# Routing made for nine tiles of two batches at once, and tail results in other PSUM banks, in a fused retention and mixture-of-experts kernel

## The chip, the cores and the metric

The kernel runs on one core of one Trainium2 chip. The metric is the device time of one execution in microseconds (us): 628.96, the median of three runs (627.0 to 629.3).

## The reference, cut to what matters

Decayed attention without a softmax over 8 batches of 8 heads (576 positions, width 64), then a layer in which every one of the 4608 tokens goes to one expert of eight:

```python
scores = scale * np.matmul(q, k.transpose(0, 1, 3, 2))
Dmat = np.where(rel >= 0, gamma[:, None, None] ** rel[None, :, :], 0.0)
attn = np.matmul(scores * Dmat[None], v)
x = attn.transpose(0, 2, 1, 3).reshape(4608, 512)
logits = (x / norm(x)) @ (emb / norm(emb)).T / tau
expert_idx = np.argmax(logits, axis=1)        # and a gate weight by softmax
h = np.maximum(x[mask] @ w1[e], 0.0)
out[mask] = gate_w[mask, None] * (h @ w2[e])  # for each expert e
```

## The kernel before

The first 170 us compute the attention, batch by batch, and route the tokens on the side; the rest are the experts, one after the other. Python loops are unrolled, and a scheduler lays out one fixed instruction order for each engine. An engine works its queue in order, so an instruction that waits holds all that stand behind it.

**A round** is here one pass `b` of the batch loop; it has four steps `p`, one for each pair of heads. The text counts a round from the end of the last tail (`emit_Ot`) to the end of the next. In each round TensorE (PE) does:

- `emit_A(b, p)`: scores of a pair, into two PSUM banks of the pool `psa` (three banks, tile `a`). VectorE (DVE) multiplies them by the causal mask and writes them to SBUF (L599, tile `raw`).
- `emit_QT` and `emit_O`: the carried state and the scores times the values, both into a bank of `pso` (two banks, tile `o`, called `PO[p]`). DVE evicts it in `emit_X` (L681, L683, L684).
- At the end of a round (`p` = 3): the next batch's first scores, `emit_At` (scores of the 64 tail positions, evicted by DVE into `pt`, L695), `emit_U` (the next batch's states, two banks, evicted by DVE into `Tst`, L627 and L629), the last `emit_O`, and `emit_Ot` (the tail's output, two half banks for even and odd pairs, evicted by L722). In the version before, `emit_At`, `emit_U` and both halves of `emit_Ot` take banks of `psm` (three banks, tile `m`).

**Routing.** 576 tokens of a batch are 4.5 tiles of 128, so an even batch has 4 tiles and an odd one 5. For each batch `route_logits`, `route_tile` (transposes, ScalarE (ACT) evicts, the rows go to DRAM) and `route_turn` run in the slots after steps 0 and 2 of the round behind it. `route_head` (six small DVE instructions: maximum, one-hot of the expert), `route_rank` (matmuls with triangle and ones, then DVE), `route_onehot` (three wide DVE instructions `ra`, `bt`, `rp`) and `route_table` (one matmul for each tile) turn logits into a table of which token lies in which slot of which expert. In the version before each of these runs once for each batch: head of batch `b` in round `b`+1, its rank, one-hots and table in round `b`+2. In round 7 a list of tasks does what is left of batches 5 and 6, and `slots_to_tokens` and three `gather`s of tokens for the first expert.

**Beside it.** GpSimd (POOL) scales the next batch's values (L567, L571) once they have landed. In rounds 2 to 5 one quarter of the first expert's weights is loaded (`wsplit_tasks`), cast by ACT (L168) and its rest formed by DVE (L169). Loads wait for free buffers; all go through the queue of SyncE.

Of the kernel before, what the change touches and what calls it, by code (L numbers as in the profile page):

```python
# [18 lines left out]
P = 128  # L19
# [6 lines left out]
NE = 8  # L26
# [60 lines left out]
def retention_moe(ctx: ExitStack, tc: tile.TileContext, qk, kv, embT, tau, w1, w2, cst, out):  # L87
# [89 lines left out]

    def group_tiles(b):
        t0 = (b // 2) * 9 + (0 if b % 2 == 0 else 4)
        return t0, (4 if b % 2 == 0 else 5)  # L180

    def route_head(b):

        t0, G = group_tiles(b)
        L = L_all[:, t0 : t0 + G, :]

        def bc(x):
            return x.unsqueeze(2).broadcast_to([P, G, NE])

        def bce(x):  # L190
            return x.unsqueeze(1).broadcast_to([P, G, NE])

        mx = sm.tile([P, 5], F32, name="mx")[:, :G]
        nc.vector.tensor_reduce(out=mx, in_=L, axis=AX.X, op=ALU.max)
        nc.vector.tensor_tensor(out=L, in0=L, in1=bc(mx), op=ALU.subtract)
        w = sm.tile([P, 5, NE], F32, name="w")[:, :G]
        nc.vector.scalar_tensor_tensor(out=w, in0=L, scalar=0.0, in1=bce(wme), op0=ALU.is_ge, op1=ALU.mult)
        wm = sm.tile([P, 5], F32, name="wm")[:, :G]
        nc.vector.tensor_reduce(out=wm, in_=w, axis=AX.X, op=ALU.max)
        oh = sm.tile([P, 5, NE], BF16, name="oh")[:, :G]  # L200
# [42 lines left out]
    def route_rank(b):  # L243
# [9 lines left out]
        mm(r, stri, oh, start=True, stop=False)  # L253
        if b > 0:
            mm(r, ones, bce(run), start=False, stop=False)
# [4 lines left out]
        nc.vector.tensor_reduce(out=s1, in_=oh.rearrange("p g e -> p e g"), axis=AX.X, op=ALU.add)  # L260
        if b == 0:
# [4 lines left out]
        t1 = sm.tile([P, 5, NE], F32, name="t1")[:, :G]  # L266
        nc.vector.tensor_tensor(out=t1, in0=r, in1=oh, op=ALU.mult)
# [5 lines left out]

        si = sm.tile([P, 5], I32, name="si")[:, :G]
# [3 lines left out]
        ai = sm.tile([P, 2, 5], I32, name="ai")[:, :, :G]  # L278
        nc.vector.tensor_scalar(out=ai[:, 0], in0=si, scalar1=7, scalar2=None, op0=ALU.logical_shift_right)
# [3 lines left out]
    def route_onehot(b):  # L283

        t0, G = group_tiles(b)
        ai = grp[b][0]
        bt = sm.tile([P, 5, P], BF16, name="bt", bufs=1)[:, :G]
        nc.vector.tensor_tensor(
# [4 lines left out]
        )  # L293
        ra = sm.tile([P, 5, NE, CT], F32, name="ra", bufs=1)[:, :G]
        held = cc("iota")[:, : NE * (CT + 1)].rearrange("p (e i) -> p e i", e=NE)[:, :, :CT]
# [5 lines left out]
        )  # L301
        rp = sm.tile([P, 5, 2, NA], BF16, name="rp", bufs=1)[:, :G]
        nc.vector.tensor_tensor(
# [7 lines left out]
    def route_table(b):  # L311
# [11 lines left out]
        u = ps[:, : 2 * NA].rearrange("p (k a) -> p k a", k=2)  # L323
        if b == 0:
# [122 lines left out]
    with ExitStack() as att:  # L447
# [238 lines left out]
        def emit_At(b):  # L686
            ps = psm.tile([P, 512], F32, name="m")
            u = ps[:, : NP * TL].rearrange("p (r n) -> p r n", r=NP)
# [44 lines left out]
        def route_tile(b, g):  # L733

            t0, G = group_tiles(b)
            src = tile_src(b, g)
# [29 lines left out]
        def route_turn(b):  # L766
            t0, G = group_tiles(b)
            lt = ltb.pop(b)
# [399 lines left out]
```

## Time and profile before

| | |
|---|---|
| median of three runs | 628.96 us (627.0 to 629.3) |
| the profiled execution, own time | 627.92 us |
| its span, first to last instruction | 626.1 us |
| PE busy | 609.4 us (97%) |
| DVE busy | 339.3 us (54%) |
| ACT, POOL busy | 216.7 us, 180.3 us |
| rounds 1 to 7 (29.16 to 166.64 us) | 137.48 us, PE busy 129.36 |
| granted TensorE clock, whole span | 0.995 of full |

Times below are us from the start of the span. A line of a timeline or of a table of waits says in brackets how long the engine sat idle in front of the instruction, and what released it. Matmul ends are modelled, so a busy PE need not be at its peak rate.

### The profile page before, as it was taken

The numbers are of one execution on the slowest core, as the hardware profiler recorded it, in microseconds if no ns is written. First come the engines' busy times: TensorE is split into PE (matmuls) and PEld (weight loads), VectorE is DVE, ScalarE is ACT, GpSimd is POOL, SyncE is SP. The second block draws the span as 40 slices with busy tenths as digits, with TensorE's granted clock in tenths as the row PEclk, the third lists the DMA queues.
The fourth block names the chain that finished last, engine by engine and source line by source line (L and its number), as shares of the span: only waits on it lengthen the run. The fifth ranks groups of instructions, "written<-read, shape, count | busy, mean of one in ns | idle before, by whom it ended". The sixth has DMA issues, their size and how long they took to land. (4 is left out here: it accounts for less than half of the span.)

```text
span 626.1 us, 12659 instructions
## 1 busy us (share of the span) xinstructions
PE 609.4 (97%) x5273; PEld 541.6 (87%) x5273; DVE 339.3 (54%) x687; ACT 216.7 (35%) x397; POOL 180.3 (29%) x165
## 2 busy tenths in 40 slices
PE   9999999989899999999999999999999999999995
PEld 8877778867698989889988998998899899889985
DVE  5676877768767776723670673368057426802200
ACT  1033333423444554423351433335143333512211
POOL 2522022220156636032313504241341324020011
PEclk9999999989999999999999999999999999999999
DMA  8899887972367895661483258147324824510001
GB/s 308 311 329 367 300 317 275 344 262 103 106 208 218 206 307 153 149 235 46 118 274 103 81 115 268 65 118 238 130 69 114 273 71 117 149 51 9 2 35 44
DMA packets 73275, 109.41 MB, mean 175 GB/s; under 512 B 44634, under 2 KB 45054, under 8 KB 71424
## 3 DMA queue, kind: packets, MB, share of 16 engines
q1 hardware_dynamic: 65536, 88.63, 44.1%
q0 software_dynamic: 7680, 19.95, 9.6%
q8 instruction: 42, 0.69, 0.4%
q14 instruction: 17, 0.14, 0.1%
HBM read 79.96 MB, written 19.94 MB: 160 GB/s over the span
## 5 line engine op out<-in xcount | busy, mean ns | idle before, releaser
L109 PE MATMUL a<-xs,wslot 128*128 128x384 f32 (+1 forms) x1536 | 227.8, 309 | 0.0
L109 PEld LDWEIGHTS a<-xs,wslot 128*128 128x128 f32 x1536 | 225.8, 189 | 0.7
L913 PE MATMUL o<-wslot,hs 128*128 128x512 f32 (+1 forms) x984 | 222.0, 386 | 0.0
L913 PEld LDWEIGHTS o<-wslot,hs 128*128 128x128 f32 x984 | 181.1, 188 | 38.3
L887 DVE SCALAR_TENSOR_TENSOR hs<-a,hs 128x384 fp32r<-128x384 f32 (+1 forms) x128 | 62.8, 490 | 170.6 <-ACT hs L886 167.8
L921 POOL DMA_INDIRECT out<-y,sid x40 | 43.4, 1086 | 225.1 <-ACT y L920 192.8
L886 ACT ACTIVATE hs<-a 128x384 fp32r<-128x384 f32 (+1 forms) x128 | 56.1, 439 | 127.3 <-PE a L109 117.3
L169 DVE TENSOR_TENSOR wslot<-raw,wslot 128x1024 fp32r<-128x1024 f32 x64 | 78.3, 1223 | 26.5 <-ACT wslot L168 25.4
L168 ACT CAST wslot<-raw 128x1024 fp32r<-128x1024 f32 x64 | 66.8, 1044 | 39.2 <-DMA raw<-w 39.2
L355 POOL DMA_INDIRECT raw<-xd,gid x40 | 41.6, 1041 | 88.8 <-DVE wslot L169 45.6
L920 ACT ACTIVATE y<-o,gt 128x512 f32<-128x512 f32 (+1 forms) x41 | 27.7, 677 | 110.5 <-PE o L913 94.7
L567 POOL TENSOR_TENSOR vt<-vt,cs 128x512 f32<-128x512 f32 x28 | 28.3, 1045 | 90.4 <-DMA vt<-kv 74.4
L366 POOL DMA_INDIRECT gt<-gd,gid x40 | 50.0, 1251 | 12.2 <-issue 12.2
L109 PE MATMUL a<-qkt 64*128 64x128 f32 x512 | 43.0, 291 | 2.5 <-DVE raw L599 2.5
L599 DVE TENSOR_TENSOR raw<-a,tri 128x512 f32<-128x512 f32 x64 | 41.4, 684 | 6.1 <-PE a L109 6.0
L109 PEld LDWEIGHTS a<-qkt 64*128 64x128 f32 x512 | 34.9, 189 | 7.5 <-DVE raw L599 3.9
L109 PE MATMUL o<-raw,vt 128*64 128x128 f32 x512 | 36.1, 280 | 0.0
L109 PEld LDWEIGHTS o<-raw,vt 128*64 128x64 f32 x512 | 28.2, 138 | 4.3 <-issue 3.2
L400 DVE COPY raw<-raw 128x1024 uint16<-128x1024 uint16 x37 | 28.2, 785 | 4.0 <-DMA raw<-raw 4.0
L744 ACT COPY y<-m 128x512 f32<-128x512 f32 x34 | 18.8, 586 | 32.5 <-PE m L113 32.4
L393 DVE COPY raw<-raw 128x1024 uint16<-128x1024 uint16 x37 | 26.0, 717 | 0.9 <-DMA raw<-xd,gid 0.9
L763 ACT COPY lt<-m 128x512 f32<-128x512 f32 (+1 forms) x12 | 5.4, 482 | 59.8 <-PE m L109 59.8
(127 smaller groups left out, 386.6 us busy)
## 6 DMA issues: line engine op xcount, KB each, us to landing
raw<-w SPq DMA_DIRECT2D x64, 512.0 KB, 4.8
qkt<-qk SPq DMA_DIRECT2D x32, 576.0 KB, 6.4
xd<-y SPq DMA_DIRECT2D x36, 256.0 KB, 3.5
vt<-kv SPq DMA_DIRECT2D x7, 1152.0 KB, 10.3
kt<-kv SPq DMA_DIRECT2D x7, 1024.0 KB, 5.0
vt<-kv SPq DMA_DIRECT2D x4, 256.0 KB
raw<-xd,gid POOLq DMA_INDIRECT x40
gt<-gd,gid POOLq DMA_INDIRECT x40
```

Of the source, the lines that this page charges most:

```text
L109: pe[:] = [nc.tensor.matmul(*args, **kw)]
L168: nc.scalar.copy(hi, raw)
L169: nc.vector.tensor_tensor(out=sl[:, 1, c * 1024 : (c + 1) * 1024], in0=raw, in1=hi.bitcast(F32), op=ALU.subtract)
L355: return nc.gpsimd.indirect_dma_start(out=t[:, :DM], out_offset=None, in_=xd[:rows, :], in_offset=bass.IndirectOffsetOnAxis(ap=gid[:, a : ...
L366: nc.gpsimd.indirect_dma_start(out=g[:, i : i + 1], out_offset=None, in_=gd[:, :], in_offset=bass.IndirectOffsetOnAxis(ap=gid[:, a : a + 1 ...
L400: nc.vector.tensor_copy(far.bitcast(U16).rearrange("p (n h) -> p h n", h=2), near.rearrange("p (h n) -> p h n", h=2))
L567: eng.tensor_tensor(out=v[:, c], in0=v[:, c], in1=g[:, c].unsqueeze(2).broadcast_to([P, H, D]), op=ALU.mult)
L599: nc.vector.tensor_tensor(out=pm[:, h], in0=ps[h].rearrange("p (c n) -> p c n", c=NCH), in1=tri.unsqueeze(1).broadcast_to([P, NCH, P]), op ...
L886: a = nc.scalar.activation(hi, ps[:, :n], AF.Relu)
L887: v = nc.vector.scalar_tensor_tensor(out=hs[:, 1, f, o : o + n], in0=ps[:, :n], scalar=0.0, in1=hi.bitcast(F32), op0=ALU.max, op1=ALU.subt ...
L913: nc.tensor.matmul(ps[:, :step], hs[:, hsp, f, i * P : (i + 1) * P], w[:, ws, f, n : n + step], start=(f == 0 and k == 0), stop=(f == NF - ...
L921: nc.gpsimd.indirect_dma_start(out=out[:, :], out_offset=bass.IndirectOffsetOnAxis(ap=sid[:, a : a + 1], axis=0), in_=y, in_offset=None, b ...
```

## The change

Batches are routed in pairs. `group_tiles` now gives the nine tiles of two batches to head, rank, one-hots and table, for batches 0 to 5; batches 6 and 7 stay single. The work that a batch does for itself (`route_tile`, `route_turn`) asks `batch_tiles`. So head runs in rounds 2, 4 and 6 for nine tiles, and rank, one-hots and table in rounds 3, 5 and 7 for nine tiles; rounds 1, 3 and 5 have no head, and rounds 2, 4 and 6 no rank, one-hots or table. The tail scores of `emit_At` take a bank of `psa`, and the odd half of `emit_Ot` one of `pso`.

```diff
+    def batch_tiles(b):
         t0 = (b // 2) * 9 + (0 if b % 2 == 0 else 4)
         return t0, (4 if b % 2 == 0 else 5)
+    def group_tiles(b):
+        return batch_tiles(b) if b >= B - 2 else ((b // 2) * 9, 9)
...
-        mx = sm.tile([P, 5], F32, name="mx")[:, :G]
+        mx = sm.tile([P, 9], F32, name="mx")[:, :G]
...
-        if b > 0:
+        if b > 1:
             mm(r, ones, bce(run), start=False, stop=False)
...
         def emit_At(b):
-            ps = psm.tile([P, 512], F32, name="m")
+            ps = psa.tile([P, 512], F32, name="a")
...
             for odd in range(2):
-                ps = psm.tile([P, 512], F32, name="m")
+                ps = pso.tile([P, 512], F32, name="o") if odd else psm.tile([P, 512], F32, name="m")
...
-            own = [lambda: route_logits(b)] + tiles[:2], tiles[2:] + [lambda: route_turn(b), head]
+            own = [lambda: route_logits(b)] + tiles[:2], tiles[2:] + [lambda: route_turn(b)] + [head] * (b % 2)
             first, second = owed or ([], [])
-            owed[:] = [rank], [table]
+            owed[:] = ([rank], [table]) if b % 2 else ()
```

The order of instructions at three places follows. On DVE, at the end of round 1, before: the head of batch 0 (`mx` to `tok_all`, and the sums `s` and `run`) stands between the logits and the first scores of batch 2 (`raw`).

```order
L776 TENSOR_REDUCE L_all<-m 128x32
L194 TENSOR_REDUCE mx<-L_all 128x4
L195 TENSOR_TENSOR L_all<-L_all,mx 128x32
L197 SCALAR_TENSOR_TENSOR w<-L_all,wme 128x32
L199 TENSOR_REDUCE wm<-w 128x4
L201 TENSOR_TENSOR oh<-wm,wme 128x32
L202 TENSOR_SCALAR tok_all<-wm 128x4
L260 TENSOR_REDUCE s_874<-oh 128x8
L262 CAST run<-s_874 128x8
L599 TENSOR_TENSOR raw<-a,tri 128x512 x2
L695 TENSOR_TENSOR pt<-m,trit 128x256
```

Scores and `pt` stand behind the whole head. The same place in the change (line numbers are four higher):

```order
L780 TENSOR_REDUCE L_all<-m 128x32
L603 TENSOR_TENSOR raw<-a,tri 128x512 x2
L699 TENSOR_TENSOR pt<-a,trit 128x256
L631 COPY Tst_196<-m 128x256
L633 TENSOR_TENSOR Tst_196<-m,Tst_196 128x256 x3
```

The eight instructions of head and sums are gone from here; scores and `pt` follow the logits at once.

On DVE at the end of round 3, in the change (before, the head of batch 2 stood between the table's eviction and L169):

```order
L780 TENSOR_REDUCE L_all<-m 128x32
L329 COPY tab<-m 128x80
L169 TENSOR_TENSOR wslot_81<-raw,wslot_81 128x1024
L603 TENSOR_TENSOR raw<-a,tri 128x512 x2
L699 TENSOR_TENSOR pt<-a,trit 128x256
L631 COPY Tst_196<-m 128x256
L633 TENSOR_TENSOR Tst_196<-m,Tst_196 128x256 x3
L687 TENSOR_TENSOR xC<-o,gsb 128x64
L688 TENSOR_TENSOR xT<-o,gsb 128x448
L726 TENSOR_TENSOR xT<-m,gsb 128x2x64
L726 TENSOR_TENSOR xT<-o,gsb 128x2x64
```

The head has left; L169 (the rest of the weights) still stands in front of the scores, `pt`, the states, the last `emit_X` and the two tail evictions, of which the second now reads a bank of `pso`.

On PE, from the end of round 4 on, before (`m_1651` are the tail scores, `m_1662` the first bank of the states, `m_1709` and `m_1710` the two halves of the tail):

```order
L109 MATMUL m_1651<-qkt_1105 64x64 [waits DVE_49]
...
L109 MATMUL m_1662<-vt_1412,kt_1414 64x64 [waits DMAHW7_49,Activation_49,Pool_49]
...
L109 MATMUL o_1559<-raw_1555,vt_1107 64x128 x8
L109 MATMUL m_1709<-qkt_1105,Tst0_196 64x64 [waits DVE_49]
L109 MATMUL m_1709<-qkt_1105,Tst0_196 64x64
L109 MATMUL m_1710<-qkt_1205,Tst0_196 64x64 [waits DVE_49,PE_49]
```

The states wait for a load, ACT and POOL, and both halves of the tail for DVE. The same place in the change (`a_1581` are the tail scores, `m_1592` the states, `m_1639` and `o_1640` the halves of the tail, `pt_1590` the masked tail scores):

```order
L109 MATMUL a_1581<-qkt_1067 64x64 [waits DVE_49]
...
L109 MATMUL m_1592<-vt_1371,kt_1373 64x64 [waits DMAHW7_49,DVE_49,Pool_49]
...
L109 MATMUL o_1495<-raw_1491,vt_1069 64x128 x8
L109 MATMUL m_1639<-qkt_1067,Tst0_196 64x64 [waits Activation_49]
L109 MATMUL m_1639<-qkt_1067,Tst0_196 64x64
L109 MATMUL o_1640<-qkt_1170,Tst0_196 64x64 x2
L109 MATMUL m_1639<-pt_1590,vt_1069 64x64 [waits DVE_49]
```

The states no longer wait for ACT, the odd half of the tail waits for no bank, and the wait for DVE has moved to the first matmul that reads `pt`.

On PE at the start of round 2, the first `emit_QT`, before (`o_811` and `o_812` are its two banks):

```order
L109 MATMUL o_812<-qkt_593,Tst0_196 64x128 [waits DVE_49,PE_49]
L109 MATMUL o_812<-qkt_593,Tst0_196 64x128
L109 MATMUL o_811<-qkt_517,Tst0_196 64x128 x2
L109 MATMUL o_812<-qkt_593,Tst0_196 64x128 x2
L109 MATMUL o_811<-raw_705,vt_519 64x128 x8
```

The only bank to be waited for was the one that is written first. The same place in the change (`o_801` and `o_802` are the two banks):

```order
L109 MATMUL o_801<-qkt_517,Tst0_196 64x128 [waits DVE_49,PE_49]
L109 MATMUL o_801<-qkt_517,Tst0_196 64x128
L109 MATMUL o_802<-qkt_593,Tst0_196 64x128 [waits DVE_49]
L109 MATMUL o_802<-qkt_593,Tst0_196 64x128
L109 MATMUL o_801<-qkt_517,Tst0_196 64x128 x2
L109 MATMUL o_802<-qkt_593,Tst0_196 64x128 x2
```

Now both banks are waited for: `o_802` is the one that the odd half of the tail has just used, and DVE must have evicted it (L726, the second). The same stands at the start of rounds 3 to 6.

## Rows read from the trace of the kernel before

**Rows 1.** The windows of the seven rounds, PE alone: window, its length, PE busy (instructions), granted TensorE clock as a share of full speed, DMA share, GB/s; the last row is the sum.

```profile
29.16:47.96 18.80, 17.35 (x321) 1.00 0.91 332
47.96:67.66 19.70, 19.10 (x340) 1.00 0.83 301
67.66:87.69 20.03, 18.33 (x330) 1.00 0.88 331
87.69:107.72 20.03, 19.11 (x341) 1.00 0.82 303
107.72:127.96 20.24, 18.33 (x330) 1.00 0.79 302
127.96:148.64 20.68, 20.32 (x341) 0.92 0.66 235
148.64:166.64 18.00, 16.82 (x263) 1.00 0.37 123
sum 137.48, PE 129.36; mean PE 18.48
```

**Rows 2.** A window in the experts' part, all engines: length, then busy time (instructions) of PE, PE's weight loads, DVE, ACT and POOL, granted clock, DMA share, GB/s.

```profile
300.00:400.00 100.00, 100.00 (x553) 90.56 (x552) 47.91 (x69) 35.52 (x59) 28.96 (x26) 1.00 0.54 155
```

**Rows 3.** What PE waited for in the seven rounds (29 to 166.7 us): the tile of the waiting matmul and its line, what released it; then us in total, times, the longest.

```profile
PE m L109 <- DVE pt L695: 2.6, 3, 1.0
PE a L109 <- DVE raw L599: 1.9, 5, 0.4
PE m L109 <- issue: 1.7, 4, 0.6
PE m L109 <- DVE Tst L629: 1.7, 3, 0.6
```

**Rows 4.** PE's timeline at the ends of rounds 1, 3 and 5, the first matmuls of `emit_Ot`: start, length, instruction, idle time in front and its releaser.

```profile
46.47 0.33 PE L109 MATMUL m<-qkt,Tst 64*64 64x64 f32 x4 [0.88 <-DVE pt L695]
...
86.20 0.33 PE L109 MATMUL m<-qkt,Tst 64*64 64x64 f32 x4 [0.75 <-DVE pt L695]
...
126.47 0.33 PE L109 MATMUL m<-qkt,Tst 64*64 64x64 f32 x4 [0.96 <-DVE pt L695]
```

**Rows 5.** DVE's instructions by shape, 30 to 150 us, one of the head: line, operation, tiles, out<-in, count | busy us, mean ns of one | idle us in front. 128x32 is a head of 4 tiles, 128x40 one of 5.

```profile
L197 DVE SCALAR_TENSOR_TENSOR w<-L_all,wme 128x32 f32<-128x32 f32 x3 | 2.5, 824 | 0.1
...
L197 DVE SCALAR_TENSOR_TENSOR w<-L_all,wme 128x40 f32<-128x40 f32 x3 | 0.6, 191 | 0.0
```

**Rows 6.** POOL's timeline in round 1, the scaling of the next batch's values.

```profile
39.92 4.05 POOL L567 TENSOR_TENSOR vt<-vt,cs 128x512 f32<-128x512 f32 x4 [15.96 <-DMA xd<-y]
```

**Rows 7.** Timelines of ACT and DVE at the end of round 3: the cast of the weights, their rest, `pt`, the evictions of the tail; and the cast in round 4.

```profile
82.31 1.05 ACT L168 CAST wslot<-raw 128x1024 fp32r<-128x1024 f32 x1 [0.77 <-DMA raw<-w]
83.39 1.23 DVE L169 TENSOR_TENSOR wslot<-raw,wslot 128x1024 fp32r<-128x1024 f32 x1
85.73 0.41 DVE L695 TENSOR_TENSOR pt<-m,trit 128x256 f32<-128x256 f32 x1
88.37 0.48 DVE L722 TENSOR_TENSOR xT<-m,gsb 128x128 f32<-128x128 f32 x2
101.69 1.05 ACT L168 CAST wslot<-raw 128x1024 fp32r<-128x1024 f32 x1 [0.85 <-DMA raw<-w]
```

**Rows 8.** PE's timeline, the first `emit_QT` of round 4.

```profile
88.78 0.34 PE L109 MATMUL o<-qkt,Tst 64*64 64x128 f32 x4
```

**Rows 9.** The timeline of SyncE's queue at the ends of rounds 2 and 3: the loads of the next queries and keys, which wait for the buffers that `emit_Ot` reads. Then two windows of PE, columns as in rows 1.

```profile
67.13 0.81 SPq L457 DMA_DIRECT2D qkt<-qk  x2
86.57 1.20 SPq L457 DMA_DIRECT2D qkt<-qk  x2
69.00:82.00 13.00, 12.60 (x187) 1.00 1.02 405
104.00:107.00 3.00, 3.00 (x84) 1.00 0.23 88
```

**Rows 10.** PE's timeline, the states (`emit_U`) at the end of round 4.

```profile
103.93 2.09 PE L109 MATMUL m<-vt,kt 128*64 128x64 f32 x64 [0.56 <-issue]
```

**Rows 11.** PE's timeline, a wait of the scores (`emit_A`) in round 6.

```profile
137.87 1.16 PE L109 MATMUL a<-qkt 64*128 64x128 f32 x14 [0.36 <-DVE raw L599]
```

**Rows 12.** PE's timeline in round 3: the rank's matmuls with `ones`, and the table's, for 5 tiles.

```profile
72.57 0.24 PE L109 MATMUL m<-oh,ones 128*128 128x32 bf16 x4
80.51 0.34 PE L109 MATMUL m<-rp,bt 128*128 128x80 bf16 x5
```

**Rows 13.** DVE's timeline in round 3, the one-hots of 5 tiles.

```profile
73.73 0.37 DVE L296 TENSOR_TENSOR ra<-ai,cs 128x200 f32<-128x200 int32 x1
74.01 0.82 DVE L288 TENSOR_TENSOR bt<-ai,cs 128x640 bf16<-128x640 int32 x1
74.75 0.57 DVE L303 TENSOR_TENSOR rp<-ra,entry 128x400 bf16<-128x400 f32 x1
```

**Rows 14.** A window in round 6, all engines, columns as in rows 2.

```profile
130.00:131.00 1.00, 1.00 (x24) 0.72 (x16) 0.95 (x2) 0.00 (x0) 0.00 (x0) 0.50 0.92 336
```

**Rows 15.** Round 7, timelines of DVE, POOL and PE: the list of slots turned into token numbers, the gather's three issues, the first transposes of gathered tokens.

```profile
160.95 0.17 DVE L340 CAST gid<-t 128x3 int32<-128x3 f32 x1
162.01 1.19 POOL L355 DMA_INDIRECT raw<-xd,gid  x1 [20.09 <-DVE raw L599]
166.64 1.39 PE L113 MATMUL m<-ident,raw 128*128 128x128 f32 x8
```

More of the change, by code (lines that the diff above doesn't have):

```diff
@@ L176, in retention_moe @@
     grp = {}
-    def group_tiles(b):
+    def batch_tiles(b):
         t0 = (b // 2) * 9 + (0 if b % 2 == 0 else 4)
         return t0, (4 if b % 2 == 0 else 5)
+    def group_tiles(b):
+        return batch_tiles(b) if b >= B - 2 else ((b // 2) * 9, 9)
     def route_head(b):
@@ L191, in bce @@
             return x.unsqueeze(1).broadcast_to([P, G, NE])
-        mx = sm.tile([P, 5], F32, name="mx")[:, :G]
+        mx = sm.tile([P, 9], F32, name="mx")[:, :G]
         nc.vector.tensor_reduce(out=mx, in_=L, axis=AX.X, op=ALU.max)
         nc.vector.tensor_tensor(out=L, in0=L, in1=bc(mx), op=ALU.subtract)
-        w = sm.tile([P, 5, NE], F32, name="w")[:, :G]
+        w = sm.tile([P, 9, NE], F32, name="w")[:, :G]
         nc.vector.scalar_tensor_tensor(out=w, in0=L, scalar=0.0, in1=bce(wme), op0=ALU.is_ge, op1=ALU.mult)
-        wm = sm.tile([P, 5], F32, name="wm")[:, :G]
+        wm = sm.tile([P, 9], F32, name="wm")[:, :G]
         nc.vector.tensor_reduce(out=wm, in_=w, axis=AX.X, op=ALU.max)
-        oh = sm.tile([P, 5, NE], BF16, name="oh")[:, :G]
+        oh = sm.tile([P, 9, NE], BF16, name="oh")[:, :G]
         nc.vector.tensor_tensor(out=oh, in0=bc(wm), in1=bce(wme), op=ALU.is_equal)
@@ L260, in route_rank @@
         nc.vector.tensor_reduce(out=s1, in_=oh.rearrange("p g e -> p e g"), axis=AX.X, op=ALU.add)
-        if b == 0:
+        if b == 1:
             nc.vector.tensor_copy(run, s1)
@@ L265, in route_rank @@
         rk = rank_all[:, t0 : t0 + G]
-        t1 = sm.tile([P, 5, NE], F32, name="t1")[:, :G]
+        t1 = sm.tile([P, 9, NE], F32, name="t1")[:, :G]
         nc.vector.tensor_tensor(out=t1, in0=r, in1=oh, op=ALU.mult)
@@ L272, in route_rank @@
         nc.vector.tensor_reduce(out=rk, in_=t1, axis=AX.X, op=ALU.add)
-        si = sm.tile([P, 5], I32, name="si")[:, :G]
+        si = sm.tile([P, 9], I32, name="si")[:, :G]
         nc.vector.scalar_tensor_tensor(
@@ L277, in route_rank @@
         )
-        ai = sm.tile([P, 2, 5], I32, name="ai")[:, :, :G]
+        ai = sm.tile([P, 2, 9], I32, name="ai")[:, :, :G]
         nc.vector.tensor_scalar(out=ai[:, 0], in0=si, scalar1=7, scalar2=None, op0=ALU.logical_shift_right)
@@ L286, in route_onehot @@
         ai = grp[b][0]
-        bt = sm.tile([P, 5, P], BF16, name="bt", bufs=1)[:, :G]
+        bt = sm.tile([P, 9, P], BF16, name="bt", bufs=1)[:, :G]
         nc.vector.tensor_tensor(
@@ L293, in route_onehot @@
         )
-        ra = sm.tile([P, 5, NE, CT], F32, name="ra", bufs=1)[:, :G]
+        ra = sm.tile([P, 9, NE, CT], F32, name="ra", bufs=1)[:, :G]
         held = cc("iota")[:, : NE * (CT + 1)].rearrange("p (e i) -> p e i", e=NE)[:, :, :CT]
@@ L301, in route_onehot @@
         )
-        rp = sm.tile([P, 5, 2, NA], BF16, name="rp", bufs=1)[:, :G]
+        rp = sm.tile([P, 9, 2, NA], BF16, name="rp", bufs=1)[:, :G]
         nc.vector.tensor_tensor(
@@ L323, in route_table @@
         u = ps[:, : 2 * NA].rearrange("p (k a) -> p k a", k=2)
-        if b == 0:
+        if b == 1:
             nc.vector.tensor_copy(tab, u)
@@ L733, in route_tile @@
         def route_tile(b, g):
-            t0, G = group_tiles(b)
+            t0, G = batch_tiles(b)
             src = tile_src(b, g)
@@ L766, in route_turn @@
         def route_turn(b):
-            t0, G = group_tiles(b)
+            t0, G = batch_tiles(b)
             lt = ltb.pop(b)
@@ L786, in route_tasks @@
         def route_tasks(b):
-            G = group_tiles(b)[1]
+            G = batch_tiles(b)[1]
             tiles = [lambda g=g: route_tile(b, g) for g in range(G)]
@@ L797, in route_tasks @@
                 t += tiles[2:] + [table, lambda: slots_to_tokens(0, 3)]
-                t += [lambda i=i: gather(0, i, group_tiles(B - 1)[0] * P) for i in range(3)]
+                t += [lambda i=i: gather(0, i, batch_tiles(B - 1)[0] * P) for i in range(3)]
                 return t + [route_bump]
```

## The prediction, blind

> **What bounds the kernel now.** I read the windows first. In the experts' part PE has no gap (100.00 busy of 100.00, clock 1.00 [rows 2]), so whatever the rounds lose or gain is carried to the end. The rounds last 137.48 us, with PE busy 129.36 of it [rows 1]; the 8.1 us between are what the change can reach, with the part of round 6 that ran at a lower clock. Next, the table of waits: four lines make nearly all of the 8.1, the tail waiting for `pt` (2.6), the tail's odd half (1.7), the states (1.7, shown as "issue") and the scores waiting for `raw` (1.9) [rows 3]. Last, the timelines of these places, to see what made the releaser late. At the ends of rounds 1, 3 and 5 PE idles 0.88, 0.75 and 0.96 us in front of `emit_Ot` [rows 4].
>
> Rounds 2 to 5 have a second limit beside PE. DMA is full for most of a round (1.02 at 405 GB/s from 69 to 82 us) and nearly idle at its end (0.23) [rows 9], because the next loads of queries and keys wait for buffers that `emit_Ot` reads. These loads are issued at 67.13 and 86.57, and the cast of the weights, which waits for its own load behind them, starts at 82.31 and 101.69 [rows 7, 9]: 15.18 and 15.12 us later, twice the same. From the cast (82.31) a solid chain of DVE runs through L169 (83.39), scores, `pt` (85.73), states and `emit_X` to the tail's eviction, which ends at 88.85, 6.54 us behind the cast [rows 7]; at 88.78 the next `emit_QT` starts [rows 8]. So a round of this kind is held by three things: PE's program, "the next `emit_QT` not before cast + 6.5", and "the cast 15.1 behind the last `emit_Ot`'s first loads".
>
> **The change part by part.** All terms are against the profiled execution, 627.92 us, which lies 1.04 below the median of 628.96.
>
> *End of round 1.* The head of 4 tiles goes from in front of `pt`. It ran beside POOL's scaling (39.92, 4.05 us in four pieces [rows 6]), and one of its operations took 824 ns, where that of 5 tiles takes 191 [rows 5]. Without it `pt` is ready before PE comes: −0.88 [rows 4]. The odd half gets a bank of its own: its wait (1.7 for three times [rows 3], 0.57 each) goes as well. There is no weight cast in this round. PE comes to the next `emit_QT` earlier by all of it: −1.45. Cover: the new wait of `emit_QT` for the odd half's eviction is hidden by the first scores of the next batch, about as long as PE ran there between tail and `emit_QT` (1.1 us, 87.69 to 88.78 [rows 1, 8]).
>
> The Trainium skill (SBUF — State Buffer, Who interferes with whom) says that a VectorE operation with two SBUF inputs and a GpSimd operation that reads SBUF take the shared port pair as an exclusive lock for a whole instruction; 824 against 191 ns agrees. By that rule a nine-tile head that met the scaling in round 6 would be held by some 0.63 us in each of its three such operations, 1.9 in all, and the sum would be −1.8 instead of −3.7; the five-tile heads of rounds 2, 4 and 6, in whose place it stands, did not meet it.
>
> *Rounds 2 to 5, PE's side.* It offers the waits for `pt` of rounds 3 and 5 (0.75, 0.96 [rows 4]) and twice 0.57 of the odd half; the states no longer wait for ACT's copy, of which 0.56 shows at the end of round 4 [rows 10]; and with no one-hots in rounds 2 and 4 the scores there don't wait for `raw` (up to 0.4 each [rows 3]). Work moves from rounds 2 and 4 to 3 and 5: rank and table of 4 tiles on PE, 0.2 + 0.25 us by the rows of 5 [rows 12], no net cost. The one-hots of 5 tiles take 0.37 + 0.82 + 0.57 = 1.76 us [rows 13]; of nine at most 9/5 of that, so DVE's block grows by up to 1.4 in rounds 3 and 5. PE has an `emit_QT` and scores between to work on; of the growth I let 0.3 in each round reach PE.
>
> *Rounds 2 to 5, the other limit.* In the round itself the gain stops at the next `emit_QT`, since L169 still stands in front of `pt`, `emit_X` and the evictions, and the cast's time in that round is given. But the tail's first matmuls no longer wait for `pt`, so buffers come free earlier, and by the constant 15.1 the next round's cast comes earlier by as much. I followed the three limits from round to round (rounds 2 to 5, all from the rows above): program lengths from `emit_QT` to the tail fall by 1.05 and 1.3 us in rounds 2 and 4 and grow by 0.75 in 3 and 5; then the start of round 3's `emit_QT` is 1.45 earlier than before, round 4's 1.9, round 5's 2.05, and that of round 6 2.65. So rounds 2 to 5 add −1.2 to the −1.45 of round 1. Bounds: 0, if loads don't follow (each gain then ends in a wait of `emit_QT`), better by no more than the whole idle time of these four rounds, 0.60 + 1.70 + 0.92 + 1.91 = 5.1 [rows 1]; above zero up to 0.5, if the wider one-hots cost PE all that isn't covered. I take the value that the constant 15.1 gives.
>
> *The clock after round 5.* Granted clock fell to 0.50, that is 1.2 of 2.4 GHz, in round 6 [rows 14] right after PE had idled 0.96 and 0.57 us at the end of round 5; over the round it is 0.92 of 20.68, a loss of 1.65 [rows 1]. Waits of nearly the same size at the ends of rounds 1 and 3 brought no fall (1.00 in rounds 2 and 4 [rows 1]). With the two waits gone I expect none, less 0.3 for a wait of `emit_QT` that takes part of their place: −1.35; bounds −1.65 and 0.
>
> *Round 6.* No cast there. The wait for `raw` goes (−0.36 [rows 11]), and rank and table of 4 tiles move to round 7 (−0.45): −0.8.
>
> *Round 7.* That −0.45 comes back: +0.45. The one-hots of nine tiles, batches 4 and 5 now together, delay the table, and the cast of the token numbers (160.95 [rows 15]) falls behind one or two evictions of scores: the gather's issues (162.01) and the first transposes of gathered tokens (166.64 [rows 15]) can come up to 1.9 us later. PE has work until then in the batch's own tail; between 0 and 1.9 I take 0.6, nearer the lower end, because DMA is at 0.37 in that round [rows 1] and the gather finds it free: +1.05 for the round.
>
> Sum: −1.45 − 1.2 − 1.35 − 0.8 + 1.05 = −3.75; 627.92 − 3.75 = 624.2, and beside the median 628.96 − 3.75 = **625.2 us**.
>
> **The rivals.** *The clock falls all the same,* or in another round. For it: the fall came at one of three like places, so its cause isn't fixed by the size of a wait. Against: the waits that stood in front of it go. Sum −2.4, 626.6 us. *Loads don't follow.* For: DMA is shared by weights, rows of x and all loads, and the queue of SyncE holds issues behind one another. Against: 15.18 and 15.12. Rounds 2 to 5 then give 0, 626.4. *All of PE's idle time goes* in rounds 2 to 5, because the cast comes far enough ahead: −5.1 in place of −1.2, 621.3. Against: the 6.5 us of DVE behind the cast stay. *The change doesn't do what it says:* `pt` is as late as before behind other DVE work, and the wait of the tail's odd half turns up as that of `emit_QT` for its eviction: 0 to +0.5, 629.0 to 629.5. For it: in rounds 3 and 5 `pt` stands behind L169, not behind the head. *Slower:* the waits at the ends of rounds become one wait of about 1.2 us in front of `emit_QT` at the start of rounds 3, 4, 5 and 6, where none stood, and the clock falls behind each. Four falls at 1.65 are 6.6; with −3.75 for the rest it is 628.96 + 2.9 = 631.8. It decides from the point where a single wait of this size brings a fall each time. Against: of three ends of rounds with 0.75 to 0.96 and 0.57, one brought a fall.
>
> The Trainium skill (TensorE: Matmul & The Clock Gate, A second HAM failure mode: psum-queue depth-cycling) reports a kernel in which short idles between groups of matmuls that cycle through PSUM banks let the clock swing; here the trace shows such idles in every round and one fall.
>
> **How the numbers follow.** Forecast 625.2 (own range 623.8 to 626.5) 0.38; clock falls all the same 0.17; loads don't follow 0.13; all idle time goes (620.5 to 623.8) 0.15; no effect 0.07; slower (630 to 634) 0.10. The range of 621.0 to 629.5 leaves out the slower case, the lower part of the case with all idle time gone and the upper edge of no effect, together 0.18. A measurement of this kernel tells about 0.5% from no change, which lies at 625.8 and 632.1. Faster than 625.8: two thirds of the forecast (0.26) and all of the 0.15, 0.41. Slower than 632.1: about half of the slower case, 0.06. The rest, 0.53, is within.
>
> **What would show it.** After round 1: no wait in front of `emit_Ot`, `emit_QT` of round 2 at 47.6 (47.96 [rows 1] and 1.1 of scores, less 1.45). Rounds 3 and 5: the tail's first matmuls without a wait, a short wait moved to those that read `pt`, and one in front of the next `emit_QT`; the loads of queries and keys earlier by 0.5 us or more, and the cast 15.1 behind them. Round 6 at clock 1.00. Round 7 a little longer than 18.0, with the gather's issues near 162.0 less the 4 to 5 us gained ahead, plus 0.6 to 1.9. I would be wrong if the cast doesn't move with the loads, if granted clock falls in any of rounds 2 to 6, or if PE waits over 1 us for gathered tokens.

## The result, and the profile after

The changed kernel takes 635.18 us (median of 9 runs, 633.62 to 652.12), the kernel before 628.96 (9 runs, 627.0 to 631.71): ratio 1.0086, interval 1.0058 to 1.0115. It is slower by 0.9 per cent; 625.2 us was forecast. The profile taken with the result came from a disturbed execution (652.12 us, mean granted clock 0.966), and so did that of the run with early pairs below; the lines here are from a second execution of the changed kernel, 635.96 us, on another chip, on which the kernel before has a median of 632.58 us and the ratio is 1.009 (1.0057 to 1.0124).

The rounds of the changed kernel, PE alone, in the columns of [rows 1] (round 7 again up to the first gathered tokens):

```profile
32.36:49.83 17.47, 17.15 (x323) 1.00 0.88 325
49.83:69.86 20.03, 18.04 (x336) 1.00 0.90 331
69.86:91.92 22.06, 21.58 (x339) 0.92 0.75 275
91.92:112.28 20.36, 18.21 (x335) 1.00 0.87 325
112.28:136.13 23.85, 21.76 (x342) 0.93 0.66 250
136.13:154.05 17.92, 17.92 (x336) 1.00 0.74 273
154.05:173.14 19.09, 16.74 (x271) 1.00 0.32 106
```

Against [rows 1], round 1 is 1.33 us shorter and round 6 2.76, as forecast in kind; rounds 2 and 4 are 0.33 longer each, rounds 3 and 5 2.03 and 3.61, and there the clock fell. Round 1 begins at 32.36 in place of 29.16. That isn't the change: the kernel with weights at step 3 (below), which has the change in it, begins round 1 at 29.18, and the kernel before with nothing but L169 held back (below) at 32.72. In the changed kernel's profile PE waits up to 1.21 us there for the first batch's queries and keys, and the clock is at 0.50 from 20 to 21 us. So comparisons go by the lengths of rounds.

What PE waited for, 29 to 175 us, columns as in [rows 3]:

```profile
PE m L109 <- DVE pt L699: 3.5, 2, 1.8
PE m L113 <- DMA raw<-xd,gid: 2.7, 2, 2.1
PE a L109 <- DVE raw L603: 1.4, 2, 1.1
PE o L109 <- DVE xT L685: 1.2, 2, 1.0
```

The three waits for `pt` of [rows 4], at the ends of rounds 1, 3 and 5, are gone; two longer ones stand at the ends of rounds 2 and 4, where there was none. The states no longer wait for ACT; instead they wait 0.32 us for POOL at the end of round 1, and the tail 0.37 for ACT at the end of round 4. New against [rows 3] are the wait of `emit_QT` for the last `emit_X`, that for gathered tokens, and a longer one for the scores' eviction. PE's timeline of these places (rounds 2 to 5):

```profile
69.35 0.27 PE L109 MATMUL m<-pt,vt 64*64 64x64 f32 x2 [1.69 <-DVE pt L699]
72.00 1.78 PE L109 MATMUL o<-qkt,Tst 64*64 64x128 f32 x24 [0.22 <-DVE xT L685]
81.29 1.16 PE L109 MATMUL a<-qkt 64*128 64x128 f32 x8 [0.26 <-DVE raw L603]
111.78 0.27 PE L109 MATMUL m<-pt,vt 64*64 64x64 f32 x2 [1.77 <-DVE pt L699]
114.43 1.94 PE L109 MATMUL o<-qkt,Tst 64*64 64x128 f32 x24 [0.98 <-DVE xT L685]
125.50 1.16 PE L109 MATMUL a<-qkt 64*128 64x128 f32 x8 [1.11 <-DVE raw L603]
```

Behind these waits the clock is at 0.50, 1.2 GHz: in round 3 from about 70.1 to 73.5 us, already before the wait of 0.22, in round 5 from 114.4 to 117.9, behind the wait of 0.98. Two windows of all engines show it (columns as in [rows 14]); the 24 matmuls of `emit_QT` that take 0.89 us in round 3 of the kernel before take 1.78 and 1.94:

```profile
72.00:73.00 1.00, 1.00 (x16) 0.89 (x20) 1.00 (x4) 0.00 (x0) 0.00 (x0) 0.50 0.94 389
...
116.00:117.00 1.00, 1.00 (x12) 0.70 (x10) 0.00 (x0) 0.00 (x0) 0.00 (x0) 0.50 0.98 395
```

By the mean clock of rounds 3 and 5 that costs, as an estimate, 22.06 × 0.08 = 1.8 and 23.85 × 0.07 = 1.7 us. Why `pt` is late is read from the end of round 2: the load of the next queries and keys on SyncE's queue, then ACT and DVE, which answer to [rows 7]:

```profile
49.58 1.39 SPq L461 DMA_DIRECT2D qkt<-qk  x2
65.03 1.05 ACT L168 CAST wslot<-raw 128x1024 fp32r<-128x1024 f32 x1 [2.63 <-DMA raw<-w]
66.11 1.23 DVE L169 TENSOR_TENSOR wslot<-raw,wslot 128x1024 fp32r<-128x1024 f32 x1 [2.83 <-ACT wslot L168]
68.00 0.22 DVE L201 SCALAR_TENSOR_TENSOR w<-L_all,wme 128x72 f32<-128x72 f32 x1
68.88 0.42 DVE L699 TENSOR_TENSOR pt<-a,trit 128x256 f32<-128x256 f32 x1
```

DVE stands idle for 2.83 us in front of L169, with scores and `pt` queued behind; the cast waits for its load. In the kernel before the load, the cast, `pt` and PE's first reader of `pt` at the end of round 2 were:

```profile
46.84 1.20 SPq L457 DMA_DIRECT2D qkt<-qk  x2
61.62 1.05 ACT L168 CAST wslot<-raw 128x1024 fp32r<-128x1024 f32 x1 [0.56 <-DMA raw<-w]
65.69 0.42 DVE L695 TENSOR_TENSOR pt<-m,trit 128x256 f32<-128x256 f32 x1
67.06 0.27 PE L109 MATMUL m<-pt,vt 64*64 64x64 f32 x2
```

Counted from the start of round 1 (29.16 and 32.36), `pt` is ready at 36.95 us before and at 36.94 in the change. PE came for it at 37.90 before; in the change it is there at 35.30 (69.35 − 1.69 − 32.36). So PE gained 2.6 us and `pt` nothing. Last, the one-hots of rounds 3 and 5 (tile shapes 128x1152 and 128x720) with POOL's scaling, from the timelines of DVE and POOL:

```profile
78.47 1.35 DVE L292 TENSOR_TENSOR bt<-ai,cs 128x1152 bf16<-128x1152 int32 x1
79.74 0.90 DVE L307 TENSOR_TENSOR rp<-ra,entry 128x720 bf16<-128x720 f32 x1
80.13 4.41 POOL L571 TENSOR_TENSOR vt<-vt,cs 128x512 f32<-128x512 f32 x4 [14.29 <-DMA vt<-kv]
121.83 1.35 DVE L292 TENSOR_TENSOR bt<-ai,cs 128x1152 bf16<-128x1152 int32 x1
123.10 1.75 DVE L307 TENSOR_TENSOR rp<-ra,entry 128x720 bf16<-128x720 f32 x1
122.19 5.56 POOL L571 TENSOR_TENSOR vt<-vt,cs 128x512 f32<-128x512 f32 x4 [14.57 <-DMA vt<-kv]
```

In round 3 the scaling starts while `rp` runs, and `rp` keeps its 0.90. In round 5 it starts while `bt` runs; `rp` then takes 1.75 in place of 0.90, the scaling 5.56 in place of 4.05 [rows 6], and PE waits 1.11 for the scores behind it.

### The profile page after: what moved, and what is told of

Same layout as the page of the kernel before. It is cut to its first block, busy times and chain, and to the rows that moved or that the text cites. A ratio compares the mean times of both kernels' runs of the same rounds, so it can differ in the third digit from the quotient of the medians.

```text
span 650.2 us, 12600 instructions
## 1 busy us (share of the span) xinstructions
PE 625.9 (96%) x5270; PEld 552.9 (85%) x5270; DVE 332.9 (51%) x636; ACT 217.2 (33%) x397; POOL 181.7 (28%) x165
## 5 line engine op out<-in xcount | busy, mean ns | idle before, releaser
L169 DVE TENSOR_TENSOR wslot<-raw,wslot 128x1024 fp32r<-128x1024 f32 x64 | 78.4, 1225 | 33.7 <-ACT wslot L168 33.7
L571 POOL TENSOR_TENSOR vt<-vt,cs 128x512 f32<-128x512 f32 x28 | 32.2, 1180 | 105.3 <-DMA vt<-kv 51.9
L109 PE MATMUL a<-qkt 64*128 64x128 f32 (+1 forms) x640 | 49.8, 282 | 6.8 <-DVE raw L603 4.5
L109 PEld LDWEIGHTS a<-qkt 64*128 64x128 f32 (+1 forms) x640 | 41.4, 183 | 12.7 <-DVE raw L603 5.2
L370 POOL DMA_INDIRECT gt<-gd,gid x40 | 47.9, 1197 | 12.2 <-issue 11.9
L109 PE MATMUL o<-raw,vt 128*64 128x128 f32 x512 | 40.0, 300 | 0.0
L109 PEld LDWEIGHTS o<-raw,vt 128*64 128x64 f32 x512 | 31.4, 149 | 5.2 <-issue 4.4
L109 PE MATMUL o<-qkt,Tst 64*64 64x128 f32 (+1 forms) x448 | 27.1, 298 | 1.8 <-DVE xT L685 1.6
```

Source lines behind the costliest of these rows:

```text
L109: pe[:] = [nc.tensor.matmul(*args, **kw)]
L169: nc.vector.tensor_tensor(out=sl[:, 1, c * 1024 : (c + 1) * 1024], in0=raw, in1=hi.bitcast(F32), op=ALU.subtract)
L370: nc.gpsimd.indirect_dma_start(out=g[:, i : i + 1], out_offset=None, in_=gd[:, :], in_offset=bass.IndirectOffsetOnAxis(ap=gid[:, a : a + 1 ...
L571: eng.tensor_tensor(out=v[:, c], in0=v[:, c], in1=g[:, c].unsqueeze(2).broadcast_to([P, H, D]), op=ALU.mult)
```

## The experiments

Three theories were tried: O, that the nine one-hots beside POOL's scaling are the loss; B, that the bank moves are; and W, that `pt` waits for the weights' L169 in the now shorter even rounds. Ratios are to the kernel before on the same chip, with 95% intervals.

**Banks alone, pairs alone.** The diff of the change, cut in two: `banks_only` has the lines of `emit_At` and `emit_Ot`, `pairs_only` all the others.

> The changed kernel once more, for a profile of a usual execution (the one at hand shows a clock of 0.966 and 650 us). Theory O (one-hots): the three one-hot instructions of nine tiles in rounds 3 and 5 run beside POOL's scaling of the values, are stretched from an estimated 3.2 us to 3.6 and over 5 us, hold the scores' eviction, PE waits 1 to 3 us, and the clock falls behind it; then these waits stand in this profile too, with one-hots and scaling side by side. Theory B (banks): the tail in other banks makes PE wait for pt (1.7 us) and then for the odd half's eviction (0.8 us) at the ends of rounds 2 and 4, and the clock falls behind these. Both: 634 to 636 us.

> The kernel before with the two bank moves alone (tail scores in psa, odd tail in pso; heads, ranks and one-hots for each batch as before). Theory O: nothing of nine tiles, so no loss: 626 to 629 us. Theory B: the loss is here: 632 to 636 us, waits for pt and in front of emit_QT at the ends of rounds 2 and 4.

> The change with the old banks (tail scores and both halves of the tail in psm), so only the routing of nine tiles at once. Theory O: the loss is here: 632 to 636 us, one-hots beside the scaling in rounds 3 and 5. Theory B: 626 to 629 us.

Measured: banks alone 630.45 us, 0.9968 (0.9942 to 0.9995); pairs alone 634.71, 1.0041 (1.0017 to 1.0066). So the banks by themselves gain a little, the loss comes in with the pairs, and the two together lose more (1.009) than the pairs alone: theory B as stated falls, although its waits for `pt` and in front of `emit_QT` stand in the changed kernel's profile. With pairs and old banks, PE waits at the same two places, only one step earlier, since the states' bank is there copied by ACT behind the cast:

```profile
68.34 1.15 PE L109 MATMUL m<-vt,kt 128*64 128x64 f32 x32 [1.73 <-ACT y L748]
...
109.81 1.15 PE L109 MATMUL m<-vt,kt 128*64 128x64 f32 x32 [2.23 <-ACT y L748]
```

In this profile the clock stayed at 1.00 in the rounds, and the one-hots didn't meet the scaling, though theory O had expected them to. So the time lies in the range that O gave for the pairs alone, but not by one-hots and scaling side by side.

**Weights at step 3.**

```diff
-                if 1 < b < 6 and p == 1 and wq:
+                if 1 < b < 6 and p == 3 and wq:
```

> The change with the first expert's weights taken at step 3 of rounds 2 to 5 in place of step 1, so that their cast and L169 stand behind pt and the states on ACT and DVE. Theory W (weights): the change is slower because its even rounds are shorter on PE, but pt must still wait for L169, and L169 for the weights' load; PE then idles 1.7 us in front of pt's readers at the ends of rounds 2 and 4 and the clock falls to 1.2 GHz behind it. Then both waits and both falls go, and the ratio to the kernel before is 0.998 to 1.002. Theory O (one-hots beside POOL's scaling): only the waits of the scores in rounds 3 and 5 count, they stay, and the ratio is 1.006 to 1.010.

> The kernel before with the two bank moves and the weights at step 3; routing for each batch as before. Theory W: with L169 behind the tail the waits in front of emit_QT at the starts of rounds 3 to 6 (0.4 to 0.9 us each in the kernel with bank moves alone, ratio 0.997) go or shrink, ratio 0.992 to 0.996. If L169 doesn't hold anything there: 0.996 to 0.998. If the later load of weights collides with the next batch's loads: above 0.998.

Measured: with the change 636.07 us, 1.0051 (1.0009 to 1.0093); with the banks alone 630.94, 0.9988 (0.9953 to 1.0024). Rounds 2 and 4 of the former took 18.43 and 18.68 us, with 0.15 left of the wait for `pt`: that part of W holds. But the ratio with the change lies between the ranges of both theories, and that with the banks alone in the range for a collision of loads. The weights now come in front of the next batch's loads, the second bank of `emit_QT` waits for the tail's eviction (1.10), and round 3 took 27.30 us, with the clock at 0.87 and the one-hots fully beside the scaling:

```profile
65.26:92.56 27.30, 23.48 (x339) 0.87 0.62 227
...
75.85 2.20 DVE L292 TENSOR_TENSOR bt<-ai,cs 128x1152 bf16<-128x1152 int32 x1
77.97 1.74 DVE L307 TENSOR_TENSOR rp<-ra,entry 128x720 bf16<-128x720 f32 x1
75.72 5.90 POOL L571 TENSOR_TENSOR vt<-vt,cs 128x512 f32<-128x512 f32 x4 [12.96 <-PE a L109]
80.37 1.16 PE L109 MATMUL a<-qkt 64*128 64x128 f32 x8 [1.95 <-DVE raw L603]
```

The edit moves the load as well, so it doesn't tell W from O cleanly; `rest_late` below does.

**One-hots in two rounds.** `late_onehot` runs `route_onehot` for tiles 4 to 8 behind the first eviction of the next round.

```diff
...
-            owed[:] = ([rank], [table]) if b % 2 else ()
+            if b % 2 and b < 5:
+                rank = lambda: (route_rank(b), route_onehot(b, 0, 4))
...
+                owed[:] = [rank], [lambda: route_table(b, 0, 4)], [late_onehot], [lambda: route_table(b, 4)]
```

> The change with head and rank of nine tiles, but one-hots and table of tiles 0 to 3 in round 3 and of tiles 4 to 8 in round 4 (batches 0 to 3; batches 4 and 5 as in the change). Theory O: the wait of the scores in round 3 goes (0.3 us), that in round 5 stays for batches 2 and 3 in halves is gone too, and the ratio falls from 1.009 to 1.004 or below. Theory W: round 4 gets 0.25 to 0.5 us of PE work back, so its wait for pt is shorter by that, the clock still falls behind rounds 2 and 4, and the ratio is 1.006 to 1.009.

Measured: 635.11 us, 1.0048 (1.0007 to 1.009), between the two theories; the interval takes in O's 1.004 and much of W's range. Scores waited 0.43 us at most and round 5 took 19.46 us in place of 23.85, which points to the one-hots, though the clock didn't fall in that round here; round 2 took 21.46, with a wait of 1.77 for ACT and the clock at 0.92.

**The kernel before, once more.**

> The kernel before once more, for a second profile: how far its first 29 us (loads of the first batch) and the clock after round 5 vary between executions. If the 3.2 us by which round 1 begins later in the changed kernel's profile come from the change, round 1 begins at 29.0 to 29.5 here; if they are chance of the first loads, anywhere from 29 to 33.

Measured: 627.42 us, one execution. Round 1 began at 30.07, the clock did not fall in round 6, and PE waited 0.74 and 0.49 us for gathered tokens, which it didn't in the first profile:

```profile
129.02:148.14 19.12, 18.77 (x341) 1.00 0.69 255
```

So the 1.35 us that the prediction took from a fall of the clock after round 5 were a chance of the one execution shown in [rows 1, 14].

**L169 alone held back.** Load and cast stay; only DVE's instruction goes behind the tail's evictions (`dv[0]` is the second L726, `hold` the list of rests).

```diff
...
+                    with after(dv[0]):
+                        while len(hold) > 1:
+                            hold.pop()()
```

> The change with L169 of the first expert's weights held back behind the tail's evictions; load and cast stay where the change has them. Theory W (pt waits for L169 at the ends of rounds 2 and 4): the waits of 1.7 us in front of pt's readers go, rounds 2 and 4 take 18.4 to 18.8 us (20.0 and 20.4 in the change), and if the clock no longer falls in rounds 3 and 5 the ratio to the kernel before comes down from 1.009 to 1.002. Theory O (one-hots of nine tiles): rounds 3 and 5 stay above 22 us with waits of the scores or a fall of the clock, whatever rounds 2 and 4 do, and the ratio stays above 1.004.

> Bank moves with routing for each batch, and L169 held back behind the tail's evictions. Theory W says that L169 holds the emit_QT of the next round through pt, the states and emit_X: the waits of 0.43 to 0.86 us in front of emit_QT at the starts of rounds 3 to 6 go, rounds 2 to 5 are shorter by 0.5 us each, ratio 0.992 to 0.996. If the loads set the pace, waits appear elsewhere and the ratio stays at 0.997.

> The kernel before with L169 held back behind the tail's evictions and nothing else: old banks, routing for each batch. If L169 in front of pt costs the kernel before as well (waits for pt of 0.64 to 0.96 us at the ends of rounds 3 and 5, and the start of the next emit_QT), the ratio is 0.993 to 0.996 and most of the 0.989 of rest_late_banks is L169's. If the old banks keep PE waiting anyway (the tail's odd half 0.55 us, the states for ACT's copy 0.3 to 0.7 us), the ratio stays at 0.997 to 1.000, and the two edits need each other.

Measured: in the changed kernel 632.32 us, 0.9966 (0.9935 to 0.9997), where the change itself is 1.009; with the bank moves alone 628.78, 0.9892 (0.9855 to 0.9929); in the kernel before alone 628.92, 0.9949 (0.9915 to 0.9982). So one instruction of 1.23 us, moved by a few places, brings the changed kernel from 1.009 to 0.9966. Not all of that was the change's loss: the same move gains 0.5 per cent in the kernel before and 0.8 with the banks alone (0.9968 to 0.9892), against 1.2 here. So some 0.5 to 0.7 per cent is the late `pt` that came with the change, a rough share, as each ratio is known to 0.3 or 0.4 per cent; and with L169 out of the way the pairs still cost 0.7 (0.9966 against 0.9892).

W had expected 18.4 to 18.8 us for rounds 2 and 4 and a ratio of 1.002, O over 22 us for rounds 3 and 5 and a ratio above 1.004; with the banks alone the gain is larger than W's range, though waits of 0.86 and 0.70 us in front of `emit_QT` stay at the starts of rounds 4 and 6. The rounds of the changed kernel with L169 held back, and its one-hots and scaling in round 3:

```profile
46.82:66.50 19.68, 18.04 (x336) 1.00 0.84 317
66.50:87.85 21.35, 20.31 (x340) 1.00 0.82 303
87.85:106.13 18.28, 18.04 (x337) 1.00 0.89 338
106.13:127.45 21.32, 20.35 (x341) 1.00 0.79 299
...
75.67 0.90 DVE L314 TENSOR_TENSOR rp<-ra,entry 128x720 bf16<-128x720 f32 x1
78.16 4.04 POOL L578 TENSOR_TENSOR vt<-vt,cs 128x512 f32<-128x512 f32 x4 [14.16 <-DMA vt<-kv]
```

The wait for `pt` is 0.21 at the end of round 2 and none at that of round 4 (round 2 has a wait of 1.43 for ACT at another place), the clock stays at 1.00 in all rounds, and the one-hots are over (76.57) before the scaling starts (78.16). So in these two profiles the falls of the clock and the meeting of one-hots and scaling go with the late `pt`. This profile is of the fastest of the kernel's 12 executions, with a mean clock of 0.994 where all twelve have 0.991, so others may have falls.

The late `pt` is about half of the loss in rounds 2 to 5. They take 86.30 us in the change and 80.63 here, 80.00 in the kernel before and 77.42 with L169 held back in it. Of the 6.3 us that the change added, 3.1 go with L169 beyond what its move gives the kernel before, and 3.2 stay, as rounds 3 and 5 remain at 21.3 us. These are single executions. From the start of the scores issued in step 2 to the next transposes, a stretch with the same matmuls, PE takes 80.85 − 75.02 = 5.83 us here,

```profile
75.02 1.16 PE L109 MATMUL a<-qkt 64*128 64x128 f32 x8
...
80.85 1.09 PE L113 MATMUL m<-ident,xT 128*128 128x128 f32 x8
```

and in the second profile of the kernel before 80.18 − 75.90 = 4.28:

```profile
75.90 0.71 PE L109 MATMUL a<-qkt 64*128 64x128 f32 x4
...
80.18 1.09 PE L113 MATMUL m<-ident,xT 128*128 128x128 f32 x8
```

That is 1.55 us more, most of it without a row of idle time. The stretch takes 5.83 or 5.84 us wherever nine one-hots end before the scaling starts (this kernel, the pairs alone) or just behind (round 3 of the change), 4.28 or 4.29 in those with five (the kernel before, the banks alone, L169 held back in either), and 4.10 in `onehot_split`, with one-hots of four tiles but a rank of nine. So the nine one-hots are the cause, not the rank. In round 5 of the change, where the two meet, it takes 6.68.

**Pairs for batches 0 to 3 alone,** without and with L169 held back.

```diff
-        return batch_tiles(b) if b >= B - 2 else ((b // 2) * 9, 9)
+        return batch_tiles(b) if b > 3 else ((b // 2) * 9, 9)
...
```

> The change with pairs for batches 0 to 3 alone; batches 4 to 7 are routed one by one as before. If round 7 loses 1.6 to 2 us because the nine one-hots delay the gather, that goes: round 7 (to the logits of the last batch) 19.0 to 19.3 us in place of 20.9, no wait of 2 us for gathered tokens; round 5 has five one-hots and takes 20 us or less. Ratio 1.003 to 1.005. If the loss in rounds 5 and 7 has another cause, they stay as in the change and the ratio at 1.009.

> The change with pairs for batches 0 to 3 alone and L169 held back, so that the clock doesn't fall in rounds 2 to 5. Against rest_late (0.9966) it differs only in batches 4 and 5. If nine one-hots in round 7 delay the gather by 1.6 to 2 us, the wait for gathered tokens is 0 to 1 us here and round 7 takes 19.0 to 19.3 us in place of 21.35; round 5 takes 19.5 to 20 in place of 21.3, round 6 some 19 in place of 17.6: ratio 0.992 to 0.995. If the delay of the gather has another cause: 0.996 to 0.998.

Measured: 1.0045 (1.0001 to 1.009) without, 0.9965 (0.9928 to 1.0001) with. What was expected of round 5 was wrong, as batches 2 and 3 have their one-hots there: it took 20.76 us with L169 held back. There the waits of 1.31 and 0.83 for gathered tokens are gone and round 7, up to the last batch's logits, takes 19.26 us in place of 21.35, which shows the pair of batches 4 and 5 as the cause; round 6 takes 19.86 in place of 17.64. The two cancel, and the ratio, above the 0.992 to 0.995 expected, doesn't tell this kernel from `rest_late`.

Waits for gathered tokens can bring the clock down, too. In `rest_late` it falls behind them, from about 166.6 to 170 us, outside the seven rounds:

```profile
167.00:168.00 1.00, 1.00 (x8) 0.50 0.00 0
```

It falls at that place in the profiles of the pairs alone, of the weights at step 3 with the change and of the one-hots in two rounds as well, all with the pair of batches 4 and 5. It doesn't in that of the change, which has this pair too, nor in any profile without it.

**The head held back, too.** The heads of batches 0, 2 and 4 go behind the second L726, like L169, and nothing is paired.

```diff
+            elif b < B - 2:
+                due.append(head)
...
+                        if p == NP - 1 and b % 2 and due:
+                            due.pop()()
```

> Bank moves with routing for each batch, and the heads of batches 0, 2 and 4 held back behind the tail's evictions. If what the change gained at the end of round 1 (1.3 us) is the head beside POOL's scaling, it is here too: round 1 takes 17.5 us (18.1 with the banks alone, 18.8 to 19.05 before), no wait for pt, and no later round is longer than in the kernel with bank moves alone: ratio 0.993 to 0.996. If the head is paid in round 2 instead (it now stands in front of the scores), round 2 is longer by 0.5 to 1 us and the ratio 0.996 to 0.998.

> Bank moves, L169 and the heads of batches 0, 2 and 4 held back behind the tail's evictions, routing for each batch. The parts measured 0.9968 (banks), 0.9954 (banks and heads) and 0.9892 (banks and L169). If they add: 0.986 to 0.989, with round 1 at 17.5 us and no wait for pt in rounds 1, 3 and 5. If the head then stands in the way of the next scores: 0.989 to 0.992.

Measured: with the banks alone 632.41 us, 0.9954 (0.9926 to 0.9983), round 1 17.75 us, but round 2 21.61 in place of 20.70 without the heads held back, with waits of 0.67 and 1.29 for ACT; with banks and L169 held back 623.07 us, 0.9856 (0.9802 to 0.9910), faster than both kernels of this case, and a little below the range expected if the parts add. Its rounds 1 to 5, without a wait for `pt` or in front of `emit_QT` up to round 6:

```profile
32.20:49.36 17.16, 16.96 (x322) 1.00 0.91 331
49.36:68.45 19.09, 18.75 (x345) 1.00 0.86 332
68.45:87.56 19.11, 18.41 (x333) 1.00 0.92 332
87.56:106.68 19.12, 18.76 (x344) 1.00 0.91 338
106.68:125.58 18.90, 18.40 (x335) 1.00 0.83 323
```

Rounds 3 and 5 take 19.11 and 18.90 us in place of 21.35 and 21.32 with pairs (`rest_late`), and up to the last batch's logits the seven rounds take 131.79 in place of 136.65. So the change's gain at the end of round 1 and in the banks is to be had without the pairs, which by themselves cost.

## Why the prediction was wrong, point by point

*End of round 1:* right. −1.45 forecast, −1.33 measured; the wait for `pt` and that of the odd half are gone. Pairing isn't needed for it: with the head held back round 1 takes 17.16 and 17.75 us (`best`, `heads_late_banks`), 17.47 in the change.

*Rounds 2 to 5:* this is the step that failed, the part "the other limit". Forecast −1.2, within −5.1 and +0.5; measured 86.30 − 80.00 = +6.3. What failed is that the cast, and with it `pt`, would come earlier by as much as PE. Of the 1.33 us that round 1 gained, the loads of the next queries and keys had only 0.46 (17.22 us behind the round's start in place of 17.68): both times they are issued 0.37 or 0.38 behind the tail's first matmul, and the wait of the odd half, which is gone, lay behind that. And the cast came 15.45 behind them, in place of 14.78. "Twice the same" held for rounds 3 and 4 alone: over rounds 2 to 5 it is 14.78, 15.18, 15.12 and 15.39 before, and 15.45, 18.48, 15.80 and 20.26 in the change, where ACT was at other work in front of the second and the fourth cast. Why 14.78 became 15.45 is not shown. So `pt` gained nothing by the end of round 2, PE 2.6 us, where 0.95 of slack had been. Instead of a short wait there are 1.69 and 1.77 us in one piece, and the clock falls behind them. Counted from the start of round 1, round 6 was forecast 2.65 us earlier and begins 4.97 later.

The limit "cast + 6.5" was too short as well: `emit_QT` of rounds 3 and 5 follows 6.97 and 6.96 behind the cast. It was taken from round 3, where all of the head stands in front of L169; in rounds 2 and 4 part of it lies between L169 and `pt` (cast to the end of `pt`: 3.83 in round 3 and 4.49 in round 2 before, 4.27 in round 2 of the change). And `emit_QT` in [rows 8] has no wait in front, so 6.5 was never seen to hold it. The prediction named L169 as the thing that stays in front of `pt`, and let the shortened rounds run into it without a price for the wait. `rest_late` shows that price: with L169 moved the waits of 1.69 and 1.77 are gone but for 0.21, the falls with them, 3.1 us of the 6.3. The other half is the one-hots, below.

*The clock:* the rival "slower", given 0.10, came about in rounds 3 and 5, of the four rounds it named, and at 631.8 its price was below the result, which is outside its 630 to 634, too. The falls of 1.8 and 1.7 are two of its four; the waits in front of them are for `pt` rather than in front of `emit_QT`. Over the executions that the second ratio is taken from (9 and 23) the mean clock is 0.988 in the change and 0.9915 before; by that, as an estimate, 2.3 of the 5.1 us between their mean times are the clock's. What the rival left out is what follows a fall: round 3's one-hots come later against the scaling, which goes by the loads of `vt`, and in round 5 the two meet. The Trainium skill (SBUF — State Buffer, Who interferes with whom) has the rule, an exclusive lock of the shared port pair; and the traces agree: an instruction that began beside the scaling was held (`bt` 1.35 to 2.20 and the scaling 4.05 to 5.90 with the weights at step 3, `rp` 0.90 to 1.75 in the change). The prediction weighed the rule for the heads, and what met the scaling were the one-hots.

*One-hots:* the block was bounded at 9/5 of 1.76, 3.17 us; in round 3 it takes from 78.02 to 80.64, 2.62. But of the growth 0.3 was let through to PE, and 1.55 is what arrives in each of rounds 3 and 5 even at full clock and without the scaling. This is the second term that failed, 2.5 us in two rounds. That `emit_QT` and scores cover it was an argument from the order, and wrong.

*The clock after round 5:* −1.35 was taken from one execution; the second profile of the kernel before has no fall there. Against that one, round 6 gains 1.2 (19.12 to 17.92), for which 0.8 was forecast without the clock.

*Round 7:* +1.05 forecast, +1.09 measured up to the first gathered tokens. The gather's first issue comes 15.23 us after the round's start in place of 13.37 ([rows 1, 15]), the upper bound of 1.9, and PE waits 2.07 us for the first tokens and again for the later ones (0.59), so that up to the last batch's logits it is +1.6 (20.92 against 19.33).

*The chances:* 0.18 outside the range doesn't follow from the cases. Slower (0.10) and the part below 621.0 of "all idle time goes" (0.02 of its 0.15) make 0.12; the rest would need most of "no effect", which ends at the bound of 629.5.

Against the second profile of the kernel before, round 1 is 1.58 us shorter, rounds 2 to 5 are 6.40 longer, round 6 is 1.20 shorter and round 7, up to the logits, 1.93 longer: 142.61 − 137.06 = +5.55 us, where 0.9 per cent of 632 is 5.7. Against the first profile it is +3.80, since its clock fell in round 6. These are single executions, and that the second agrees so well is in part luck. How a wait's length decides on a fall isn't settled: the pairs with old banks waited 1.73 and 2.23 us at these places, and no fall followed.

## What to carry to other kernels

An in-order engine's slack is that of its latest input: before work is taken out of a round, look for the instruction that waits for a load and stands in front of the round's last step, and move that first. Work made in one larger piece on an engine that evicts for another has to be priced at the place where the other engine stands behind it, not by its sum. A cure that is tried on the changed kernel has to be tried on the kernel before, too: here about 0.5 of its 1.2 per cent was there to be had all along. And two profiles of the kernel before tell which stalls and clock falls are its own and which are chance.

## What the runs showed of the hardware

DVE's one-hots and POOL's scaling hold each other by whole instructions. One that was running when the scaling began kept its time (`rp` 0.90 in round 3 of the change, `bt` 1.35 in round 5); one that began beside it took much longer (`rp` 1.74 or 1.75, `bt` 2.20). And the clock's fall doesn't go by the size of a wait alone: in the changed kernel 1.69 us brought it, and 1.77 with 0.98 behind it; with the old banks 1.73 and 2.23, each with 0.82 behind it, didn't. Waits of 1.31 and 0.83 for gathered tokens brought it in `rest_late`; 2.07 and 0.59 in the change didn't.
